# Seven fp64 weight slices get their sign and top exponent bits from ScalarE, and the last expert's 88-row block moves to fourth place

## The chip, the cores and the metric

One core of a Trainium2 chip runs the whole kernel as one program. The metric is the device time of one execution in microseconds (us). A profiled execution has beside it a span, from its first to its last instruction; the profile's times count from the start of the span.

The engines of the core are TensorE (PE, with its weight loads as PEld), VectorE (DVE), ScalarE (ACT), GpSimd (POOL) and SyncE (SP, which here only issues DMAs). Each runs its own instructions in order and waits on semaphores for the others.

## The reference

Three layers follow each other on 2304 tokens of width 512: attention through 32 landmarks with six Newton steps, a dense feed-forward layer with ELU, and a mixture of 8 experts of which each token uses two.

```python
def sm(a, b): ...                      # softmax(scale * a @ b.T)
A = sm(q, k_lm); Bm = sm(q_lm, k_lm); C = sm(q_lm, k)
Z = Bm.transpose(0, 1, 3, 2) / (norm1(Bm) * norminf(Bm) + 1e-06)
for _ in range(6):
    Z = 2 * Z - Z @ Bm @ Z
x = tokens_by_features(A @ Z @ C @ v)            # 2304 x 512
h = x @ w_in                                     # 512 x 2048
x = where(h > 0, h, exp(min(h, 0)) - 1) @ w_out  # 2048 x 512
top2, top2_w = softmax of the two best of x @ w_gate + log1p(exp(x @ w_noise)) * noise
out[mask] += top2_w[mask, k] * (relu(x[mask] @ w1[e]) @ w2[e])   # for e in 8, k in 2
```

w_in and w_out arrive as fp64. The kernel has them as pairs of 32-bit words and makes fp32 numbers of them by bit operations, then splits these into two f16 halves.

## The kernel before

**Order of the work.** Attention of the four batches, the dense layer, the routing and expert 0 are issued from ORDER (L51), a list of tokens written out by hand: each token issues one small step, and each engine executes its instructions in the order in which the tokens issue them. `do` (L1273) reads it. The experts 1 to 7 follow from loops.

**The fp64 slices.** w_in comes in 16 slices of 128x512 numbers (tokens `wi.j` load, `I.j.part` convert), w_out in 16 (`Wl.k` loads, `Wa.k.part` converts, `Wb` splits into f16). `bits32` (L253) gives four parts: part 0 is a ScalarE pass over the low words, which scales them by 2^-29 to integers of three bits (L258, shown as L215, the line of the helper `act`); part 1 is a VectorE pass that shifts the high words left by 3 and masks them into a temporary (L259); part 2 is a second VectorE pass that puts the sign and the top exponent bits from the high word's upper end onto that (L260); part 3 is a GpSimd add of high and low (L261). `wout_a` (L273) and `conv_wi` (L1241) call it. In the profile the tiles are named wi (w_in's slice; wi10 is feature block 1, row block 0) and win (its result), wo and woc (w_out's slice and its temporary), wout (its f16 halves).

**What stands around it.** In the same stretch ScalarE makes the transposed q and k (tile T, from PSUM xp), the landmark means (lm, lT), the exponentials (E, from pc and the maxima mx), and moves between the Newton steps (R). `gmm` (L645, PSUM pg) ends the attention of the first head group; the dense layer's products (L678) follow and keep PE filled from there on.

**The last expert.** Each expert has up to 600 rows, in five blocks: four of 128 and one of 88 (CAP is 600). `e2_mm` (L1154) makes a block's second product in PSUM ey, `e2_rest` (L1192) finishes it. A full block is 24 matmuls of 128x128 weights by 512 columns (L1161). The 88-row block is cut in thirds of 32, 32 and 24 rows, each with a matmul of 384 columns (L1164) and one of 128 (L1167): 144 matmuls and as many weight loads. For expert 7, `last_base` (L1210) first copies the accumulated result to the output (out_dram<-acc, issued by SP) and gathers the rows that expert 7 will change (base<-acc,tk, five DMAs issued by POOL). A `drain` of GpSimd stands ahead of its blocks (L1328). Then the blocks go in the order 4, 0, 1, 2, 3, where 4 is the 88-row block (L1329). Of a full block VectorE makes weight times product plus base (L1199); of the 88-row block ScalarE scales in four passes and VectorE adds the base (L1202). POOL then writes one element as a spacer (L1203) and scatters the rows into the output (L1204). PSUM ey has three buffers.

```python
for j, more in zip((0, 1, 2, 3, 4) if not last else (4, 0, 1, 2, 3), side):
    e2_mm(e, j)
    for g, *a in more:
        g(*a)
    e2_rest(e, j)
```

Of the kernel before, what the change touches and what calls it, by code (L numbers as in the profile page):

```python
# [61 lines left out]
0:asmul.0.G 0:asmax.1 nz.1.0 0:etrans.2 I.6.3 0:uout.2 wi.10 0:etout.0 0:assub.1.V 0:sqout.3 0:asback.0 0:nm.3 0:etout.1
0:uout.3 Wl.7 0:etout.2 I.7.2 0:sqout.4 I.1.2 0:asexp.1 0:nm.4 I.8.0 1:q.1 nz.0.1 0:ashi.0 0:sqout.5 0:cssum I.5.3
Wa.2.1 0:cv cl I.8.1 0:uout.4 Wa.3.2 Wa.2.0 Wa.2.2 wi.14 Wb.1.0.V Wb.1.1.V Wa.2.3 wi.15 I.7.0 0:umm.5 0:assum.1 wi.11
0:cvout I.9.0 1:v 0:uout.5 Wb.5.1.V I.1.3 0:asmul.1.G Wb.0.0.V 0:ybd.V Wa.7.0 1:lmmm.0.0 Wb.2.0.V 0:asback.1 1:xhi.0.0
0:zcv Wa.3.3 I.10.0 I.7.3 0:zout wi.12 1:xlo.0.0 I.8.2 I.15.0 1:lmmm.0.1 0:gmm.0 1:xhi.0.1 0:ashi.1 0:aslo.0.G 1:lmadd.0
F.14 0:ghi.0.0 Wa.7.1 0:aslo.1.G F.8 0:glo.0.0 0:ghi.0.1 0:glo.0.1 Wb.3.0.G I.11.1 L1.0.0 L1.0.1 0:gmm.1 Wa.7.2
1:xlo.0.1 X.0.0 T.0.0.A X.0.1 T.0.1.A I.11.0 1:k.0 Wa.7.3 S.0.0 Wl.8 H.0.0 0:ghi.1.0 L1.0.3 Wb.0.1.V S.0.1 nz.3.1
Wb.2.1.V O.0.0.V H.0.1 nz.0.3 I.10.1 I.9.3 I.11.2 0:ghi.1.1 O.0.1.V 1:xhi.1.0 0:glo.1.0 1:xtr.0.0 L1.0.2 L2.0.0.3 X.0.3
X.0.2 L2.0.0.1 1:xlo.1.0 T.0.2.A T.0.3.A L2.0.0.0 S.0.2 L2.0.0.2 L2.0.1.0 L2.0.1.1 L2.0.1.3 I.11.3 I.8.3 1:lhi.0  # L70
0:glo.1.1 I.13.0 S.0.3 L1.0.4 I.10.2 Wb.7.0.V L1.0.5 Wb.3.1.G 1:llo.0 1:ltr.0 H.0.3 O.0.3.V H.0.2 1:lmsum.1.0.V 1:k.1
L2.0.3.2 X.0.4 O.0.2.G nz.0.2 L2.0.1.2 I.15.1 I.14.1 L2.0.3.0 L2.0.2.1 T.0.4.A Wl.6 Wa.6.1 L2.0.3.1 X.0.5 S.0.4
1:lcp.0.A 1:xtr.1.0 L2.0.3.3 T.0.5.A Wb.7.1.V S.0.5 Wl.9 I.10.3 0:gmm.2 1:lmsum.1.1.V L1.0.6 H.0.4 consts O.0.4.G Wa.6.0
L1.0.7 Wa.6.2 H.0.5 L2.0.2.3 O.0.5.G X.0.6 1:xhi.1.1 0:ghi.2.0 T.0.6.A X.0.7 Wa.8.1 Wa.8.0 Wa.6.3 L2.0.2.0 L2.0.4.2
L2.0.4.1 I.14.0 0:glo.2.0 L2.0.5.0 S.0.6 Wa.8.2 Wb.6.0.V nz.3.0 1:xlo.1.1 L2.0.2.2 I.12.0 L2.0.4.3 1:xtr.1.1 L2.0.4.0
0:ghi.2.1 0:glo.2.1 T.0.7.A Wa.8.3 1:lhi.1 S.0.7 L1.0.8 H.0.7 H.0.6 1:llo.1 Wa.9.1 1:csmm.0 O.0.7.G L2.0.5.2 Wl.10
# [5 lines left out]
1:y0 Wa.12.1 L2.0.9.3 1:sqout.0 I.13.3 Wa.10.1 Wa.10.2 Wa.12.2 T.0.11.A L2.0.9.0 Wa.10.0 T.0.10.A 0:gmm.3 Wa.13.1 S.0.10
0:ghi.3.1 0:ghi.3.0 L2.0.8.1 L2.0.9.2 L2.0.8.3 0:glo.3.0 1:xtr.0.1 Wa.11.0 L2.0.8.2 1:nm.0 0:glo.3.1 Wa.12.3 Wa.10.3
S.0.11 H.0.10 Wl.15 Wa.13.2 1:uout.0 L1.0.13 H.0.11 1:sqout.1 Wb.12.0.G O.0.10.G 1:asmm.1 1:asmax.0 Wb.10.0.V L1.0.12
1:astr.1 O.0.11.G 1:assub.0.V 1:nm.1 1:cssum Wa.11.1 Wb.10.1.V 1:sqout.2 Wa.11.2 1:cv Wl.14 Wa.11.3 Wa.13.3 1:uout.1
1:asmax.1 X.0.12 Wb.12.1.G X.0.13 1:asexp.0 1:nm.2 T.0.12.A L2.0.10.3 Wb.11.0.G 1:sqout.3 fill.0 L2.0.10.2 2:k.0 nz.2.0
1:assub.1.V 1:uout.2 L2.0.10.1 1:asexp.1 L2.0.10.0 T.0.13.A 1:nm.3 1:assum.0 1:sqout.4 S.0.12 Wa.15.1 S.0.13 L1.0.15
1:uout.3 1:asmul.0.G Wb.11.1.G 1:cvout L1.0.14 1:nm.4 H.0.12 1:sqout.5 1:assum.1 2:q.0 L2.0.8.0 L2.0.11.3 Wa.15.2
O.0.12.V Wa.14.1 Wa.15.0 Wb.13.0.V L2.0.12.1 1:uout.4 X.0.14 3:k.0 1:asmul.1.V L2.0.12.3 1:umm.5 Wa.14.2 Wb.13.1.V
H.0.13 Wa.14.0 L2.0.12.0 L2.0.12.2 1:uout.5 Wa.14.3 1:ybd.A 2:q.1 1:asback.1 1:zcv T.0.14.A Wb.14.0.G S.0.14 1:zout  # L90
L2.0.11.1 O.0.13.G L2.0.13.2 Wa.15.3 L2.0.11.0 1:asback.0 L2.0.11.2 H.0.14 1:ashi.0 1:gmm.0 X.0.15 1:aslo.0.V 1:ashi.1
# [1333 lines left out]
```

## Time and profile before

| what | value |
|---|---|
| timed runs | 780.41, 784.45, 786.57 us |
| their median | 784.45 us |
| profiled execution, its own time | 779.94 us |
| its span | 778.3 us |
| what lies around the span | 1.64 us |
| granted TensorE clock over the span | 0.987 of full speed |
| PE busy | 754.0 us, 97% |
| DVE, ACT, POOL busy | 79%, 55%, 36% |

A timeline row gives the start, the duration, the engine and line, the operation with its tiles and shapes, how many instructions run together in the row, and in brackets how long the engine had been idle before and what ended that. "issue" there means that nothing in the profile held the engine back. A windows row gives for a stretch the length, the busy time and number of instructions of each engine, the granted clock, the mean busy share of the 16 DMA engines and their GB/s. A waits row gives the total, the number of times and the longest.

### The profile page before, as it was taken

To read this page: it belongs to the slowest core of one execution; us is meant where nothing else is said; L and a number is where in the kernel's file an instruction comes from. 1 tells how busy PE (TensorE), PEld (TensorE's weight loads), DVE (VectorE), ACT (ScalarE), POOL (GpSimd) and SP (SyncE) were. 2 spreads that over 40 slices of the span, in tenths; PEclk is the share of its full clock that TensorE was granted. 3 is DMA by queue.
4 is the path that set the end of the run, shared out by engine and by line. 5 is a ranking of instruction groups with operands and counts; after the bars stand their busy time and mean duration, and the time that the engine had idled before them with its cause. 6 is when DMAs were issued, how large, how long until landed. Compare 5 with 4: busy or idle time off the path is not lost. (4 is left out here: it accounts for less than half of the span.)

```text
span 778.3 us, 17519 instructions
## 1 busy us (share of the span) xinstructions
PE 754.0 (97%) x6961; PEld 445.0 (57%) x6962; DVE 618.4 (79%) x1352; ACT 427.1 (55%) x820; POOL 281.9 (36%) x302
## 2 busy tenths in 40 slices
...
GB/s 346 265 294 208 173 237 189 185 178 221 110 246 92 190 28 163 124 110 77 100 55 178 117 252 84 230 103 117 226 42 247 96 202 139 71 198 40 145 189 65
DMA packets 136200, 123.19 MB, mean 158 GB/s; under 512 B 102891, under 2 KB 105963, under 8 KB 136016
## 3 DMA queue, kind: packets, MB, share of 16 engines
...
q8 instruction: 56, 0.92, 0.5%
q14 instruction: 32, 0.26, 0.1%
...
## 5 line engine op out<-in xcount | busy, mean ns | idle before, releaser
L718 PE MATMUL y<-wout,g 128*128 128x512 f16 x864 | 205.7, 380 | 0.3 <-DVE g L711 0.2
L1161 PE MATMUL ey<-w,eh 128*128 128x512 f16 x768 | 169.1, 382 | 3.4 <-issue 3.4
L1187 POOL DMA_INDIRECT acc<-eo,tk x35 | 74.2, 2121 | 202.1 <-ACT eo L215 90.5
L718 PEld LDWEIGHTS <-g 128*128 128x128 f16 x864 | 80.7, 98 | 93.8 <-issue 9.0
L1161 PEld LDWEIGHTS <-eh 128*128 128x128 f16 x768 | 75.4, 98 | 94.0 <-issue 6.1
L678 PE MATMUL h<-AT,G 128*128 128x192 f16 (+3 forms) x768 | 108.1, 287 | 1.4 <-DVE e L706 1.2
L711 POOL TENSOR_TENSOR g<-e,g 128x384 f16<-128x384 f32 (+2 forms) x44 | 43.8, 996 | 130.7 <-ACT g L215 116.8
L678 PEld LDWEIGHTS <-G 128*128 128x128 f16 x768 | 63.7, 98 | 43.1 <-issue 5.8
L215 ACT ACTIVATE eh<-c 128x300 f16<-128x300 f32 x112 | 47.7, 453 | 61.1 <-DVE c L1083 60.7
L215 ACT ACTIVATE g<-e 128x384 f16<-128x384 f32 (+2 forms) x96 | 49.4, 519 | 45.9 <-PE y L718 27.1
L215 ACT ACTIVATE e<-h 128x384 f32<-128x384 f32 (+2 forms) x96 | 46.3, 487 | 39.1 <-PE h L678 26.2
L215 ACT ACTIVATE eo<-ey,ws 128x512 f32<-128x512 f32 (+3 forms) x60 | 32.5, 541 | 64.0 <-PE ey L1161 50.9
L706 DVE SCALAR_TENSOR_TENSOR e<-e,h 128x384 f32<-128x384 f32 (+2 forms) x96 | 52.2, 549 | 16.6 <-ACT e L215 14.0
L903 POOL DMA_INDIRECT xs<-rows,pos x36 | 36.9, 1025 | 58.2 <-DVE mcum L887 26.9
L942 DVE SCALAR_TENSOR_TENSOR w<-ew,w 128x1024 f16<-128x1024 f32 x36 | 44.6, 1261 | 14.7 <-ACT w L215 14.7
L1066 PE MATMUL eb<-tx,wpC 128*128 128x300 f16 x336 | 47.4, 291 | 0.0
L1095 DVE SCALAR_TENSOR_TENSOR eh<-c,eh 128x300 f16<-128x300 f32 x112 | 46.2, 466 | 1.0
L711 DVE TENSOR_TENSOR g<-e,g 128x384 f16<-128x384 f32 (+2 forms) x52 | 29.5, 572 | 13.2 <-ACT g L215 13.1
L1066 PEld LDWEIGHTS <-wpD 128*128 128x128 f16 x336 | 32.8, 98 | 10.8 <-issue 0.7
L1066 PEld LDWEIGHTS <-wpB 128*128 128x128 f16 x336 | 32.9, 98 | 10.0
L1066 PEld LDWEIGHTS <-wpC 128*128 128x128 f16 x336 | 32.8, 97 | 10.1
L215 ACT ACTIVATE w<-ew 128x1024 f16<-128x1024 f32 x36 | 37.0, 1050 | 0.2
...
## 6 DMA issues: line engine op xcount, KB each, us to landing
...
wi<-in_moe_w_in_dram SPq DMA_DIRECT2D x16, 512.0 KB, 10.3
...
v<-in_v_dram SPq DMA_DIRECT2D x4, 1152.0 KB, 12.1
out_dram<-acc SPq DMA_DIRECT2D x1, 4608.0 KB, 19.6
...
```

Of the source, the lines that this page charges most:

```text
L215: return A.activation(o, i, f, **kw)
L678: T.matmul(p[:, c0:c0 + n], GT[b, f // 8][:, g, x, fs], AT[b][:, g, y, o:o + n], start=(i == 0), stop=(i == 5))
L706: V.scalar_tensor_tensor(x[1], x[1], x[2], x[0], op0=ALU.mult, op1=ALU.max)
L711: e.tensor_tensor(out=HT[c, f][:, 1], in0=x[1], in1=HT[c, f][:, 0], op=ALU.subtract)
L718: T.matmul(YP[c, t], h[:, x, 128 * t:128 * t + 128], WOUT[f][:, y], start=(f == 0 and i == 0), stop=(f == 15 and i == 2))
L903: n = nc.gpsimd.indirect_dma_start(out=xs[:, :], out_offset=bass.IndirectOffsetOnAxis(ap=R["pos"][:, i // 2, i % 2:i % 2 + 1], axis=0), in ...
L942: V.scalar_tensor_tensor(dst[1][:, ks, :], t, scale, dst[0][:, ks, :], op0=ALU.mult, op1=ALU.subtract)
L1066: T.matmul(p, w_op(e, w, s, k, f), x_op(e, x, t, k), start=(i == 0 and k == 0), stop=(i == 2 and k == 1))
L1095: V.scalar_tensor_tensor(lo, o, 0.0, hi, op0=ALU.max, op1=ALU.subtract)
L1161: T.matmul(p, EH[e, f][:, x, 128 * j:128 * j + 128], W2T[e][y][:, f, :], start=start, stop=stop)
L1187: nc.gpsimd.indirect_dma_start(out=acc[:, :], out_offset=bass.IndirectOffsetOnAxis(ap=TK[e][:live(j), j:j + 1], axis=0), in_=EO[e, j], in_ ...
```

## The change

Two things change. In `bits32`, a slice whose part 0 is called with the argument A gets two more ScalarE passes on the same slice. All three now write 16-bit halves: the low pass writes the lower half of the low word; the two others take the upper half of the high word, cut it with a scale, a bias and rounding to its two top bits, scale them back and write them to the upper half of the low word. The VectorE pass of part 1 then writes its result in place of the high word (for w_out) or into the result (for w_in), with no temporary, and part 2 isn't issued. GpSimd's add is the same. Seven slices are called so: I.2, I.3, I.5 and I.6 of w_in, Wa.0, Wa.1 and Wa.5 of w_out. So ScalarE gets 14 passes more, VectorE 7 fewer; PE, POOL and SP have as many instructions as before. Some tokens of the slices stand elsewhere in ORDER. Besides, the last expert's blocks go in the order 0, 1, 2, 4, 3.

```diff
@@ ORDER, one line of it before and after @@
-0:xtp.1.0.1 0:lmmm.0.1 0:xtp.0.0.2 Wa.4.2 I.0.2 0:xth.0.0.0 I.2.0 0:lmadd.0 I.0.0 0:xth.1.0.2 I.6.1 0:xtp.0.0.1 I.3.1
+0:xtp.1.0.1 0:lmmm.0.1 0:xtp.0.0.2 Wa.4.2 I.0.2 0:xth.0.0.0 I.2.0.A 0:lmadd.0 I.0.0 0:xth.1.0.2 I.6.1 0:xtp.0.0.1 I.3.1
...
@@ bits32 @@
-        return (lambda: act(lo, lo.bitcast(U32), scale=2.0 ** -29),
-                lambda: V.tensor_scalar(tmp, hi, 3, 0x3FFFFFF8, op0=ALU.logical_shift_left, op1=ALU.bitwise_and),
+        x = t.bitcast(U16).rearrange("p (n t) -> p n t", t=4)
+        base = [hi]
+
+        def top():
+
+            act(x[:, :, 1], x[:, :, 3], scale=2.0 ** -14, bias=2.0 ** -15 - 0.5)
+            act(x[:, :, 1], x[:, :, 1], scale=2.0 ** 14)
+
+        def low(e=V):
+            act(lo if e is V else x[:, :, 0], lo.bitcast(U32), scale=2.0 ** -29)
+            if e is A:
+                top()
+                base[0] = hi if dst is None else dst
+
+        return (low,
+                lambda: V.tensor_scalar(base[0] if tmp is None else tmp, hi, 3, 0x3FFFFFF8, op0=ALU.logical_shift_left, op1=ALU.bitwise_and),
                 lambda: V.scalar_tensor_tensor(hi, hi, -0x40000000, tmp, op0=ALU.bitwise_and, op1=ALU.bitwise_or),
-                lambda: G.tensor_tensor(out=hi if dst is None else dst, in0=hi, in1=lo, op=ALU.add)), hi.bitcast(F32)
+                lambda: G.tensor_tensor(out=hi if dst is None else dst, in0=base[0], in1=lo, op=ALU.add)), hi.bitcast(F32)
@@ wout_a; conv_wi gets *e in the same way @@
-    def wout_a(kk, part):
+    def wout_a(kk, part, *e):
         if kk not in WOF:
-            WOF[kk], x = bits32(WO[kk], None, sf.tile([128, 512], I32, tag="cv", bufs=CVB, name=f"woc{kk}"))
+            WOF[kk], x = bits32(WO[kk], None, None if e else sf.tile([128, 512], I32, tag="cv", bufs=CVB, name=f"woc{kk}"))
             WO[kk] = x
-        WOF[kk][part]()
+        WOF[kk][part](*e)
@@ the last expert's blocks @@
-        for j, more in zip((0, 1, 2, 3, 4) if not last else (4, 0, 1, 2, 3), side):
+        for j, more in zip((0, 1, 2, 3, 4) if not last else (0, 1, 2, 4, 3), side):
```

On ScalarE, in the first part, before: the stretch from the second slice of w_in that is converted there (wi10, wi01) past the softmax of the first batch (BB, E) and the transposed queries (T).

```order
L215 ACTIVATE wi10_207<-wi10_207 128x512 [waits DMAHW4_49]
L215 ACTIVATE wi01_135<-wi01_135 128x512 [waits DMAHW7_49]
L215 ACTIVATE T101_261<-xp0111_285 128x384 [waits PE_49]
L215 ACTIVATE BB0_310<-BB0_310 128x64 [waits DVE_49]
L215 ACTIVATE wi10_207<-wi10_207 128x512 [waits DMAHW1_49]
L215 ACTIVATE wout1_346<-wo4_141 128x512 [waits Pool_49]
L215 ACTIVATE E00_358,cs0_357<-pc000_299,mx00_332 128x3x3x32 [waits DVE_49,PE_49]
L215 ACTIVATE E00_358,cs0_357<-pc001_300,mx00_332 128x3x3x32 [waits PE_49]
L215 ACTIVATE T001_366<-xp0010_336 128x384 [waits DMAHW0_49,PE_49]
L215 ACTIVATE wo0_223<-wo0_223 128x512 [waits DMAHW2_49]
L215 ACTIVATE T101_261<-xp0110_328 128x384
L215 ACTIVATE wo5_325<-wo5_325 128x512 [waits DMAHW7_49,Activation_49]
```

The same place now:

```order
L216 ACTIVATE wi10_209<-wi10_209 128x512 [waits DMAHW4_49]
L216 ACTIVATE wi01_135<-wi01_135 128x512 [waits DMAHW7_49]
L216 ACTIVATE wi01_135<-wi01_135 128x512 [waits Activation_49] x2
L216 ACTIVATE T101_260<-xp0111_284 128x384 [waits PE_49]
L216 ACTIVATE BB0_311<-BB0_311 128x64 [waits DVE_49]
L216 ACTIVATE wi10_209<-wi10_209 128x512 [waits DMAHW1_49]
L216 ACTIVATE wi10_209<-wi10_209 128x512 [waits Activation_49] x2
L216 ACTIVATE wout1_349<-wo4_141 128x512 [waits Pool_49]
L216 ACTIVATE E00_361,cs0_360<-pc000_300,mx00_335 128x3x3x32 [waits DVE_49,PE_49]
L216 ACTIVATE E00_361,cs0_360<-pc001_301,mx00_335 128x3x3x32 [waits PE_49]
L216 ACTIVATE T001_369<-xp0010_339 128x384 [waits DMAHW0_49,PE_49]
L216 ACTIVATE wo5_328<-wo5_328 128x512 [waits DMAHW7_49]
```

Two pairs of passes have come in, behind wi01's and the second wi10's, each pass waiting for the one ahead of it; the pass of wo0 has left this place (it now stands earlier, ahead of lm), and two more passes follow wo5's.

On VectorE, at the end of the program, before: the last expert's adds of product and base, by block (eo7_4 is the 88-row block).

```order
L1202 TENSOR_TENSOR eo7_4_10433<-eo7_4_10433,base4_9985 88x512 [waits DMASW7_49,DMASW4_49,Activation_49]
L1199 SCALAR_TENSOR_TENSOR eo7_0_10468<-ey7_0_10443,ws7_9345,base0_9977 128x512 [waits DMASW0_49,DMASW6_49,DVE_49,PE_49]
L1199 SCALAR_TENSOR_TENSOR eo7_1_10499<-ey7_1_10474,ws7_9345,base1_9979 128x512 [waits DMASW5_49,DMASW1_49,PE_49]
L1199 SCALAR_TENSOR_TENSOR eo7_2_10530<-ey7_2_10505,ws7_9345,base2_9981 128x512 [waits DMASW2_49,DVE_49,PE_49]
L1199 SCALAR_TENSOR_TENSOR eo7_3_10561<-ey7_3_10536,ws7_9345,base3_9983 128x512 [waits DMASW6_49,DMASW3_49,PE_49]
```

And now:

```order
L1214 SCALAR_TENSOR_TENSOR eo7_0_10317<-ey7_0_10292,ws7_9349,base0_9981 128x512 [waits DMASW7_49,DMASW0_49,PE_49]
L1214 SCALAR_TENSOR_TENSOR eo7_1_10348<-ey7_1_10323,ws7_9349,base1_9983 128x512 [waits DMASW1_49,DVE_49,PE_49]
L1214 SCALAR_TENSOR_TENSOR eo7_2_10379<-ey7_2_10354,ws7_9349,base2_9985 128x512 [waits DMASW5_49,DMASW2_49,PE_49]
L1217 TENSOR_TENSOR eo7_4_10530<-eo7_4_10530,base4_9989 88x512 [waits DMASW3_49,DMASW4_49,DVE_49,Activation_49]
L1214 SCALAR_TENSOR_TENSOR eo7_3_10565<-ey7_3_10540,ws7_9349,base3_9987 128x512 [waits DMASW6_49,DMASW3_49,PE_49]
```

The 88-row block's add has moved from first to fourth, as have its products on PE, its four passes on ScalarE and its scatter on POOL; which add waits for an earlier scatter (the DMASW semaphores besides its own base) has moved with it.

## Rows read from the trace of the kernel before

**Rows 1.** The page's first part: busy time, share, instructions of each engine.

```profile
PE 754.0 (97%) x6961; PEld 445.0 (57%) x6962; DVE 618.4 (79%) x1352; ACT 427.1 (55%) x820; POOL 281.9 (36%) x302
```

**Rows 2.** Waits of PE: the longest.

```profile
PE ey L1161 <- issue: 3.4, 1, 3.4
```

**Rows 3.** Timeline of the last expert's blocks.

```profile
746.74 0.39 PE L1161 MATMUL ey<-w,eh 128*128 128x512 f16 x1
746.85 1.70 ACT L215 ACTIVATE eo<-ey,ws 88x384 f32<-88x384 f32 x4 [2.43 <-PE ey L1167]
...
750.58 22.36 PE L1161 MATMUL ey<-w,eh 128*128 128x512 f16 x95 [3.44 <-issue]
...
754.22 18.23 PEld L1161 LDWEIGHTS <-eh 128*128 128x128 f16 x85 [0.16 <-issue]
754.30 0.69 DVE L1202 TENSOR_TENSOR eo<-eo,base 88x512 f32<-88x512 f32 x1 [9.37 <-issue]
...
758.47 0.09 POOL L1203 MEMSET spacer<- 1x1 f32 x1 [18.63 <-issue]
...
762.79 0.75 DVE L1199 SCALAR_TENSOR_TENSOR eo<-ey,ws,base 128x512 f32<-128x512 f32 x1 [4.60 <-DMA out_dram<-eo,tk]
...
772.98 0.75 DVE L1199 SCALAR_TENSOR_TENSOR eo<-ey,ws,base 128x512 f32<-128x512 f32 x1 [4.43 <-PE ey L1161]
774.01 0.98 POOL L1204 DMA_INDIRECT out_dram<-eo,tk  x1 [4.15 <-DVE eo L1199]
```

**Rows 4.** Windows: the 88-row block, the pause behind it, and what follows.

```profile
742.60:746.74 4.14, 4.14 (x145) 4.03 (x145) 2.19 (x6) 0.83 (x2) 0.00 (x0) 1.00 1.17 364
746.74:750.50 3.76, 0.39 (x3) 0.10 (x1) 0.00 (x0) 1.66 (x4) 0.00 (x0) 1.00 0.67 211
750.50:754.30 3.80, 3.72 (x10) 1.41 (x11) 0.00 (x0) 0.00 (x0) 0.00 (x0) 0.55 0.34 123
```

**Rows 5.** The page's DMA queues: packets, MB, share; one of the instruction queues.

```profile
q8 instruction: 56, 0.92, 0.5%
```

**Rows 6.** DMA queues and transfers from 726 to 747.5 us, all kinds.

```profile
q1 hardware_dynamic: 95, 4.67, 62.8%
q0 software_dynamic: 199, 0.39, 11.9%
q14 instruction: 3, 0.02, 0.4%
issues: line engine op xcount, KB each, median us to landing
out_dram<-acc SPq DMA_DIRECT2D x1, 4608.0 KB, 19.6
base<-acc,tk POOLq DMA_INDIRECT x5, 17.9
```

**Rows 7.** The same view from 747.5 to 749 us.

```profile
q8 instruction: 1, 0.02, 3.7%
```

**Rows 8.** Groups of ScalarE, 0 to 50 us, shapes apart: busy, mean ns.

```profile
L215 ACT ACTIVATE wi<-wi 128x512 int32<-128x512 uint32 x10 | 6.7, 692 | 5.1 <-DMA wi<-in_moe_w_in_dram 5.1
...
L215 ACT ACTIVATE ET<-pe 96x512 f32<-96x512 f32 x3 | 1.7, 591 | 0.0
```

**Rows 9.** The same for VectorE.

```profile
L260 DVE SCALAR_TENSOR_TENSOR wi<-wi,win 128x512 int32<-128x512 int32 x9 | 6.5, 725 | 0.0
```

**Rows 10.** Timeline of the first part: where ScalarE waits, and the first gmm.

```profile
13.50 0.68 ACT L215 ACTIVATE wo<-wo 128x512 int32<-128x512 uint32 x1 [1.66 <-DMA wo<-in_moe_w_out_dram]
...
21.32 0.42 ACT L215 ACTIVATE lm<-k 128x256 f32<-128x256 f32 x1 [3.42 <-DVE k L345]
...
25.36 0.26 ACT L215 ACTIVATE BB<-BB 128x64 f32<-128x64 f32 x1 [0.54 <-DVE BB L452]
...
27.73 0.65 ACT L215 ACTIVATE E<-pc,mx 128x288 f32<-128x288 f32 x1 [0.97 <-DVE mx L518]
...
34.48 0.22 ACT L215 ACTIVATE R<-nb 128x64 f32<-128x64 f32 x1 [1.16 <-DVE R L571]
...
44.32 0.69 ACT L215 ACTIVATE wi<-wi 128x512 int32<-128x512 uint32 x1 [1.06 <-DMA wi<-in_moe_w_in_dram]
...
54.14 1.09 PE L645 MATMUL pg<-win,Z 64*32 64x512 f32 x16
```

More of the change, by code (lines that the diff above doesn't have):

```diff
@@ L62 @@
[L62 to L76, printed above, removed]
@@ L82 @@
[L82 to L91, printed above, removed]
@@ new lines @@
+wi.14 Wb.1.0.V Wb.1.1.V Wa.2.3 wi.15 I.7.0 0:umm.5 0:assum.1 wi.11 0:cvout I.9.0 1:v 0:uout.5 Wb.5.1.V I.1.3 0:asmul.1.G
+Wb.0.0.V 0:ybd.V Wa.7.0 1:lmmm.0.0 Wb.2.0.V 0:asback.1 1:xhi.0.0 0:zcv Wa.3.3 I.10.0 I.7.3 0:zout wi.12 1:xlo.0.0 I.8.2
+I.15.0 1:lmmm.0.1 0:gmm.0 1:xhi.0.1 0:ashi.1 0:aslo.0.G 1:lmadd.0 F.14 0:ghi.0.0 Wa.7.1 0:aslo.1.G F.8 0:glo.0.0
+0:ghi.0.1 0:glo.0.1 Wb.3.0.G I.11.1 L1.0.0 L1.0.1 0:gmm.1 Wa.7.2 1:xlo.0.1 X.0.0 T.0.0.A X.0.1 T.0.1.A I.11.0 1:k.0
+Wa.7.3 S.0.0 Wl.8 H.0.0 0:ghi.1.0 L1.0.3 Wb.0.1.V S.0.1 nz.3.1 Wb.2.1.V O.0.0.V H.0.1 nz.0.3 I.10.1 I.9.3 I.11.2
@@ new lines @@
+0:ghi.1.1 O.0.1.V 1:xhi.1.0 0:glo.1.0 1:xtr.0.0 L1.0.2 L2.0.0.3 X.0.3 X.0.2 L2.0.0.1 1:xlo.1.0 T.0.2.A T.0.3.A L2.0.0.0
+S.0.2 L2.0.0.2 L2.0.1.0 L2.0.1.1 L2.0.1.3 I.11.3 I.8.3 1:lhi.0 0:glo.1.1 I.13.0 S.0.3 L1.0.4 I.10.2 Wb.7.0.V L1.0.5
+Wb.3.1.G 1:llo.0 1:ltr.0 H.0.3 O.0.3.V H.0.2 1:lmsum.1.0.V 1:k.1 L2.0.3.2 X.0.4 O.0.2.G nz.0.2 L2.0.1.2 I.15.1 I.14.1
+L2.0.3.0 L2.0.2.1 T.0.4.A Wl.6 Wa.6.1 L2.0.3.1 X.0.5 S.0.4 1:lcp.0.A 1:xtr.1.0 L2.0.3.3 T.0.5.A Wb.7.1.V S.0.5 Wl.9
+I.10.3 0:gmm.2 1:lmsum.1.1.V L1.0.6 H.0.4 consts O.0.4.G Wa.6.0 L1.0.7 Wa.6.2 H.0.5 L2.0.2.3 O.0.5.G X.0.6 1:xhi.1.1
@@ new lines @@
+T.0.9.A L2.0.7.1 1:bnorm L1.0.10 Wl.12 Wb.9.1.V 1:csexp.1 L2.0.6.2 S.0.9 I.14.3 1:nmm H.0.8 I.12.3 1:etrans.0 1:nval
+L2.0.6.1 Wa.12.0 1:etrans.1 L1.0.11 Wl.13 H.0.9 1:etout.1 1:etout.0 O.0.9.V Wb.8.1.V Wa.13.0 I.13.2 X.0.11 L2.0.9.1
+I.15.3 1:etrans.2 O.0.8.G 1:sqmm.0 1:etout.2 X.0.10 1:y0 Wa.12.1 L2.0.9.3 1:sqout.0 I.13.3 Wa.10.1 Wa.10.2 Wa.12.2
+T.0.11.A L2.0.9.0 Wa.10.0 T.0.10.A 0:gmm.3 Wa.13.1 S.0.10 0:ghi.3.1 0:ghi.3.0 L2.0.8.1 L2.0.9.2 L2.0.8.3 0:glo.3.0
+1:xtr.0.1 Wa.11.0 L2.0.8.2 1:nm.0 0:glo.3.1 Wa.12.3 Wa.10.3 S.0.11 H.0.10 Wl.15 Wa.13.2 1:uout.0 L1.0.13 H.0.11
@@ new lines @@
+X.1.1 T.1.1.V 2:xhi.0.1 S.1.1 1:glo.1.0 H.1.1 L2.0.15.1 O.1.1.G L2.0.15.0 1:glo.1.1 L2.0.15.2 YA.0.0 L1.1.2 YA.0.2
+L2.0.15.3 S.1.0 1:gmm.2 X.1.2 YV.0.2 T.1.2.A S.1.2 H.1.0 L1.1.4 O.1.0.V 1:ghi.2.0 2:k.1 YV.0.0 2:lmsum.1.1.G H.1.2 X.1.4
+O.1.2.V T.1.4.A L1.1.5 L2.1.0.0 1:ghi.2.1 S.1.4 L2.1.0.1 H.1.4 1:glo.2.0 L1.1.3 X.1.3 fill.2 2:xtr.1.0 YA.0.1 YA.0.3
+2:lhi.0 L2.1.2.1 1:glo.2.1 O.1.4.V 1:gmm.3 T.1.3.V L2.1.2.0 S.1.3 YV.0.3 H.1.3 X.1.5 L1.1.6 YV.0.1 2:llo.0 L2.1.4.1
+T.1.5.A 2:lmsum.1.0.G S.1.5 L2.1.4.0 O.1.3.G nz.0.0 X.1.6 RT.0.0 L2.1.1.1 T.1.6.V L1.1.8 1:ghi.3.1 H.1.5 1:ghi.3.0
@@ new lines @@
+L2.2.8.1 L2.2.10.1 L1.2.13 X.2.11 2:uout.3 2:sqout.4 L2.2.9.2 3:llo.0 T.2.11.A S.2.11 2:nm.4 H.2.12 2:asback.0 2:uout.4
+2:sqout.5 facc.2 L2.2.9.0 2:umm.5 L2.2.10.0 L1.2.14 H.2.11 2:uout.5 O.2.12.G 2:ashi.0 2:ybd.V 2:zcv O.2.11.V L2.2.11.2
+PD.0.7 X.2.13 2:zout L2.2.12.0 2:gmm.0 X.2.14 3:xtr.1.0 2:ghi.0.1 L2.2.11.0 2:assum.1 T.2.14.A 2:asmul.1.V 3:ltr.0
+T.2.13.V 3:lmsum.1.1.G RS.1.0 S.2.13 L2.2.10.2 L2.2.11.1 2:asback.1 2:aslo.0.V 2:ghi.0.0 H.2.13 L2.2.12.2 2:ashi.1 3:v
+3:lcp.0.A S.2.14 2:glo.0.0 L1.2.15 PD.1.6 H.2.14 2:aslo.1.G 2:glo.0.1 O.2.14.V 3:csmm.0 O.2.13.G L2.2.12.1 X.2.15
@@ new lines @@
+3:etout.0 L1.3.5 L2.3.1.2 3:etout.1 X.3.4 T.3.4.V L2.3.2.2 L2.3.1.1 2:gmm.2 S.3.4 L1.3.6 RG.2 H.3.4 O.3.3.G RS.1.2
+2:ghi.2.1 2:glo.2.1 O.3.4.V 3:llo.1 L2.3.2.1 RA.2 L2.3.3.2 X.3.6 L2.3.3.1 T.3.6.V X.3.5 3:ltr.1 2:ghi.2.0 L2.3.4.0
+3:xtr.0.1 T.3.5.V P.0.0.0 L2.3.2.0 S.3.6 3:cv RB.2 3:lcp.1.A 3:bmm L1.3.7 3:xlo.0.0 RC.2 S.3.5 H.3.5 3:cvout P.0.7.0
+2:glo.2.0 3:bmax O.3.5.V 3:bex X.3.7 T.3.7.A 2:gmm.3 L2.3.5.2 RD.2 3:bnorm L2.3.3.0 L2.3.4.1 S.3.7 3:nmm L1.3.9
+3:xtr.0.0 2:ghi.3.1 RE.2 PD.1.2 H.3.7 L2.3.4.2 O.3.7.V L2.3.7.2 2:ghi.3.0 2:glo.3.0 3:nval RK.2 RF.2 H.3.6 2:glo.3.1
@@ new lines @@
+3:sqout.5 3:uout.4 L2.3.8.0 3:umm.5 H.3.12 S.3.11 H.3.11 L1.3.14 3:assub.0.V O.3.11.G L1.3.13 3:uout.5 3:ybd.A L2.3.9.0
+3:asexp.0 3:asmul.1.G 3:zcv O.3.12.G L2.3.9.2 L2.3.11.1 X.3.13 3:assum.0 3:asback.1 3:zout T.3.13.A 3:gmm.0 3:ashi.1
+S.3.13 L2.3.11.2 H.3.13 X.3.14 O.3.13.V 3:ghi.0.0 L2.3.12.1 T.3.14.V 3:asmul.0.G 3:asback.0 L2.3.11.0 L2.3.12.2
+3:ghi.0.1 RS.2.3 3:ashi.0 3:aslo.1.V 3:aslo.0.V L2.3.12.0 L1.3.15 X.3.15 S.3.14 3:glo.0.0 H.3.14 L2.3.13.2 O.3.14.G
+T.3.15.A 3:glo.0.1 3:gmm.1 RS.2.2 L2.3.14.0 S.3.15 L1.4.1 3:ghi.1.0 L2.3.14.1 3:ghi.1.1 L1.4.0 H.3.15 X.4.0 T.4.0.V
```

189 lines of the change are left out of this document (90 added, 99 removed).

## The prediction, on record before the run

> **What bounds the kernel now.** I read the page's first part first: PE is busy for 754.0 of the span's 778.3 us [rows 1], so only what makes PE wait, or runs behind its last product, can move the end. The waits of PE come next. The longest of the whole program is 3.4 us put down to "issue", on L1161, the last expert's second products [rows 2]; that is one of the two places that the change touches. The timeline shows it: the 88-row block's products end, one product of block 0 runs at 746.74, and the next 95 start at 750.58 after 3.44 us of idle [rows 3]. ScalarE's four passes on the 88-row block are done by 748.55, and nothing in the kernel makes block 0's second product wait for them.
>
> What PE lacks there I take to be its own code. Queue q8 moved 0.92 MB in 56 packets [rows 5], 16.4 KB each; PE's 6961 + 6962 instructions [rows 1] over 56 are 249 per packet, so I read q8 as PE's code. From 726 to 747.5 us the list of queues has no q8 at all, while the copy out_dram<-acc of 4608 KB took 19.6 us to land [rows 6] and the DMA engines stood at a share of 1.17 [rows 4]. One q8 packet came between 747.5 and 749 [rows 7], and PE ran again at 750.58. The 88-row block is hungry: it and the first product used 145 matmuls and 145 loads, 290 instructions, in 4.14 us [rows 4], where a full block has 48 in some 5 us. [...]
>
> **The tail, step by step.** At full clock 85 products took 18.23 us, 0.2145 each; 95 would take 20.38, and took 22.36 [rows 3]. So the pause costs 3.44 and the slow clock behind it 1.98, together 5.42 us. In the new order blocks 0, 1 and 2 come first: 144 instructions in 72 x 0.2145 = 15.44 us, so until 742.60 + 15.44 = 758.04. The code on hand reached 290 instructions past 742.60; 146 of these are left for the 88-row block, used up at about 758.04 + 146/290 x 4.14 = 760.1. The packet that came late for 746.74 lies well ahead of that, with the copy over at about 752. I therefore take pause and slow clock as gone: PE ends at 742.60 + 4.14 + 96 x 0.2145 = 767.3, some 0.2 more for the joints, against 772.94. That is **-5.4 us**.
>
> What could be late next: block 0's add needs its gathered base; the 88-row block's add in the old order started at 754.30, behind the last of the gathers [rows 3, 6], so none comes later than that. Block 4 is the fourth to use one of three PSUM buffers, and block 0's is free by 754.30 + 0.75 = 755.1, ahead of 758.04. POOL's first spacer comes at 758.47 in either order (the drain ahead of it), and the add that waits for the first scatter's landing then comes at 762.79 [rows 3]; in the new order that is block 2's, 4.6 us ahead of PE's end. The 88-row block ends on PE at 762.4; 1.70 us of ScalarE and 0.69 of VectorE [rows 3] bring it to about 765, its scatter to 766.2, and block 3's scatter, the last, is due at 768.5. So the last block still sets the end and is a full one as before: 0.75 us of add, 0.98 of scatter, and what follows [rows 3], unchanged.
>
> **The front, step by step.** Seven VectorE passes go, 725 ns each in w_in's group [rows 9]: 7 x 0.725 = 5.1 us of VectorE, which nothing on PE waited for, so I count them at nothing; were they on the path, that would be the gain. The cost is ScalarE's: 14 passes more. Their form, 16-bit elements 8 bytes apart, is in no row. The nearest is the low pass itself, 4-byte elements 8 bytes apart, 692 ns [rows 8]; as each pass waits for the one ahead of it, I put them 0.71 apart. Below, I take 591 ns, the shortest row of 512 elements [rows 8]; above, twice the 692, 1.38, should half words written into a word cost a pass of their own. I take 0.71, near the nearest row.
>
> Slice I.2's two passes lie ahead of the wait at 13.50 (1.66 us idle), and Wa.0's three in the 3.42 us of idle ahead of lm at 21.32 [rows 10]: nothing, though the latter only if its slice has landed by about 19 us; at twice the price they would end a good 1 us late. The other five slices bring ten passes between 23.2 and 34.5 us, where ScalarE is nearly full: 10 x 0.71 = 7.1, less 0.7 for Wa.0's first pass, which has left this stretch. Of these 6.4 us the waits there swallow 0.54 (BB), 0.97 (E) and 1.16 (R, a Newton step) [rows 10], together 2.67. What is left, 3.7, moves the Newton steps, whose products PE can't start earlier, and is cut once more by the 1.06 us that ScalarE waits for a slice's DMA at 44.32 [rows 10]: 2.7. Two VectorE instructions now queue behind ScalarE's longer series (Wa.5's shift, the f16 split of w_out); behind them stand the next Newton operations, for a few tenths. I take **+3.0 us** at gmm (54.14 [rows 10]); from there PE is filled, and the delay is carried to the end. At 0.591 the same sum gives 5.9 - 0.7 - 2.67 - 1.06 = +1.5, at 1.38 it gives 13.8 - 4.4 = +9.4.
>
> [...]
>
> **The sum.** -5.4 + 3.0 = -2.4 us: the profiled execution would go from 779.94 to 777.5. That execution is the lowest of four; the three timed ones are 780.41, 784.45 and 786.57, so a median of a few runs lies higher. I put -2.4 on the median of all four, (780.41 + 784.45) / 2 = 782.4: **780.0 us**.
>
> **Rivals.**
>
> *A: the pause stays.* If it is not the code's lateness but something that comes with the switch from 288 narrow products to full ones, or if half of the 88-row block, now in fourth place, finds its code missing in turn, the 5.4 us are not gained, only moved. For it: the pause stands right at that switch, and the trace has no line that names its cause. Against it: the seven earlier experts have the same block and no such wait among PE's, and q8's one packet fits. Then only the front counts: 782.4 + 3.0 = 785.4.
>
> [...]
>
> *B: the half-word passes are dear.* Writing 16 bits into 32-bit words costs ScalarE twice: +9.4 at the front, - 5.4 at the tail, so slower, 782.4 + 4.0 = 786.4. For it: no row shows such a pass, and a series in which each waits for the last. Against it: the strided pass of 4 bytes costs no more than other passes. It decides from 10p - 4.4 = 5.4, so from 0.98 us per pass.
>
> *C: the front costs nothing.* PE's waits in the first 55 us have other causes too, DMAs among them, and VectorE, freed of 5.1 us, reaches its own steps earlier. For it: ScalarE's waits for DMAs at 13.50 and 44.32 [rows 10]. Against it: ten passes between 23 and 34.5 us, where ScalarE waits for 2.67 us in all. Then -5.4 alone: 777.0.
>
> **How the numbers follow.** Forecast 0.55, A 0.17, B 0.10, C 0.18. The range: C's 777.0 less the spread of runs at the lower end, B's 786.4 with it at the upper, so 772 to 788. A measurement of this kernel can tell about 1%, 7.8 us, from no change; most of the forecast, all of A and most of B lie within. Faster by more than 1% needs C, or the forecast with the spread on its side: 0.17. Slower by more needs B with the spread: 0.06. Same: 0.77.
>
> **What would show it.** Right: in the changed profile PE has no "issue" wait on L1176 (the new number of L1161's line), the granted clock of the tail is 1.00, and PE's last product ends some 5.3 us before the span does, as now; ten passes of about 0.7 us more between 23 and 38 us on ScalarE; gmm at about 57.1 instead of 54.14. Wrong: a pause within or behind the 88-row block (A); half-word passes at 1 us or more and gmm beyond 60 (B); gmm at 54 to 55 (C); or POOL's or VectorE's last wait ending on a scatter instead of PE.

## The result, and the profile after

The changed kernel took 793.97 us (median of four, 792.93 to 794.48), the kernel before beside it 782.61 us: a ratio of 1.0145, 95% interval 1.0108 to 1.0183. So it is slower by some 11 us, where the prediction said 2.4 us faster on a median of 782.4, with 788 as the upper end. In the profiles the span went from 778.3 to 792.5 us.

The waits of PE in the changed kernel (total, times, longest), for the one row of [rows 2]:

```profile
PE xp L412 <- ACT T L216: 5.6, 2, 3.4
PE pa L438 <- ACT T L216: 4.0, 1, 4.0
...
PE pe L550 <- ACT E L216: 2.3, 1, 2.3
...
PE l1b L377 <- ACT lm L216: 1.4, 1, 1.4
...
PE ey L1182 <- issue: 0.7, 2, 0.4
```

The 3.4 us of "issue" on the last expert are gone. In their place stand waits on ScalarE, 13.3 us together in the first four rows, all in the first 55 us; before, only the wait for E was among them, with 0.9 us. What ScalarE did there shows in its groups from 0 to 56 us, shapes apart (busy, mean ns, idle before), which answer to [rows 8]:

```profile
L216 ACT ACTIVATE wi<-wi 128x512 uint16<-128x512 uint16 x8 | 10.8, 1346 | 0.3
L216 ACT ACTIVATE wo<-wo 128x512 uint16<-128x512 uint16 x6 | 8.1, 1344 | 0.2
...
L216 ACT ACTIVATE wi<-wi 128x512 uint16<-128x512 uint32 x4 | 5.4, 1350 | 2.9 <-DMA wi<-in_moe_w_in_dram 2.9
L216 ACT ACTIVATE wo<-wo 128x512 uint16<-128x512 uint32 x3 | 4.1, 1356 | 1.1 <-DMA wo<-in_moe_w_out_dram 1.1
...
L216 ACT ACTIVATE wi<-wi 128x512 int32<-128x512 uint32 x3 | 2.1, 704 | 0.0
```

The 14 added passes took 1.35 us each, not 0.71. And the low pass of the seven slices, which the change did not add but made to write 16 bits, went from 0.69 to 1.35 as well; the slices that still write 32 bits are at 0.70. So 21 passes are dear, not 14.

The timeline of the same stretch shows a slice holding ScalarE for 4.1 us, and the Newton step R behind it starting with no idle time of ScalarE ahead of it, where [rows 10] has 1.16 us; then the first product of gmm, which stood at 54.14:

```profile
40.19 4.09 ACT L216 ACTIVATE wo<-wo 128x512 uint16<-128x512 uint32 x3
...
44.99 4.10 ACT L216 ACTIVATE wi<-wi 128x512 uint16<-128x512 uint32 x3
48.84 0.30 ACT L216 ACTIVATE R<-nb 128x64 f32<-128x64 f32 x1
...
67.15 1.09 PE L660 MATMUL pg<-win,Z 64*32 64x512 f32 x16
```

So gmm is 13.0 us late. At the other end, the timeline of the last expert, for [rows 3]:

```profile
760.59 15.70 PE L1176 MATMUL ey<-w,eh 128*128 128x512 f16 x72
...
778.25 0.11 PEld L1182 LDWEIGHTS <-eh 128*32 128x32 f16 x2 [0.29 <-issue]
...
778.98 0.23 PE L1182 MATMUL ey<-w,eh 128*32 128x128 f16 x1 [0.35 <-issue]
...
779.71 0.23 PE L1182 MATMUL ey<-w,eh 128*32 128x128 f16 x1 [0.35 <-issue]
...
781.83 5.35 PE L1176 MATMUL ey<-w,eh 128*128 128x512 f16 x24
```

The windows of blocks 0 to 2, of the 88-row block and of block 3 (columns as in [rows 4]):

```profile
760.40:776.20 15.80, 15.80 (x75) 7.09 (x73) 4.30 (x10) 0.99 (x3) 0.09 (x1) 1.00 0.53 173
776.20:781.80 5.60, 4.83 (x145) 4.04 (x144) 0.71 (x1) 0.00 (x0) 2.17 (x4) 1.00 0.25 97
781.80:787.20 5.40, 5.38 (x26) 2.27 (x24) 0.73 (x2) 1.66 (x4) 2.13 (x4) 1.00 0.26 82
```

The clock stays at 1.00, and from the first product to the end of the last the expert takes 787.18 - 760.59 = 26.6 us, against 772.94 - 742.60 = 30.3 before. But the 88-row block takes 5.6 us instead of 4.14: PE halts three times in its middle, and no wait on another engine stands ahead of a halt. The two ends make 13.0 - 3.7 = +9.3 of the span's 14.2 us; the remaining 4.9 lie between gmm and the last expert (688.5 us before, 693.4 after). The runs below show that the passes do not make these.

### The profile page after: what moved, and what is told of

Same layout as the page of the kernel before. It is cut to its first block, busy times and chain, and to the rows that moved or that the text cites. A ratio compares the mean times of both kernels' runs of the same rounds, so it can differ in the third digit from the quotient of the medians.

```text
span 792.5 us, 17527 instructions
## 1 busy us (share of the span) xinstructions
PE 758.0 (96%) x6961; PEld 446.5 (56%) x6962; DVE 615.0 (78%) x1345; ACT 449.4 (57%) x834; POOL 282.4 (36%) x302
## 5 line engine op out<-in xcount | busy, mean ns | idle before, releaser
L1176 PE MATMUL ey<-w,eh 128*128 128x512 f16 x768 | 167.4, 379 | 0.0
L216 ACT ACTIVATE e<-h 128x384 f32<-128x384 f32 (+2 forms) x96 | 46.5, 487 | 40.3 <-PE h L693 26.6
```

The lines of the kernel that those rows point to most:

```text
L216: return A.activation(o, i, f, **kw)
L1176: T.matmul(p, EH[e, f][:, x, 128 * j:128 * j + 128], W2T[e][y][:, f, :], start=start, stop=stop)
```

## The experiments

Theory T: the ScalarE passes cost the front some 13 us because of their price, and the block order gains by itself.

**e1_order_alone.** The block order without the passes:

```diff
-        for j, more in zip((0, 1, 2, 3, 4) if not last else (4, 0, 1, 2, 3), side):
+        for j, more in zip((0, 1, 2, 3, 4) if not last else (0, 1, 2, 4, 3), side):
```

> Only the last expert's block order of the change (0, 1, 2, 4, 3), no ScalarE pass added. Theory T: the block order gains by itself, because PE no longer stands for 3.4 us behind the 88-row block and no half-clock stretch follows; in the changed kernel the last expert's products took 26.6 us instead of 30.3, so about 4 us faster than before, 778 to 779 where before has 782.6, the profile's span near 774; a remainder of the pause (0.5 to 2 us) inside the 88-row block. Rival U: the gain in the changed kernel came from the late start of its last expert (other transfers beside it), the block order alone gains nothing: within 1 us of before.

774.22 us beside 777.56 (another chip, on which the kernel before takes 5 us less): ratio 0.9957, interval 0.9931 to 0.9982. The order gains 0.43%, 3.3 us, alone; U falls. In its profile the windows of blocks 0 to 2, the 88-row block and block 3 show no halt at all, 25.1 us together:

```profile
740.40:756.10 15.70, 15.70 (x74) 6.98 (x72) 3.87 (x8) 0.83 (x2) 0.00 (x0) 1.00 0.57 186
756.10:760.20 4.10, 4.10 (x145) 4.03 (x144) 0.00 (x0) 0.00 (x0) 1.64 (x4) 1.00 0.06 19
760.20:765.70 5.50, 5.42 (x29) 2.27 (x24) 1.48 (x3) 1.66 (x4) 3.04 (x6) 1.00 0.39 143
```

A packet on q8 starts at 745.74 here, 5.3 us after the expert's first product and so hardly sooner than before (748.24 against 742.61, 5.6 us). PE doesn't stand for it: until then it has met only full blocks, 48 instructions in 5.2 us each, where the 88-row block has 288 in 4.1.

**e2_passes_alone.** The changed kernel with the blocks in the old order (4, 0, 1, 2, 3).

> Only the ScalarE passes of the change, the last expert's blocks in the old order (4, 0, 1, 2, 3). Theory T: the passes alone cost 13 us up to the first gmm, some 2 us where ScalarE stands before a transposed landmark copy near 190 us, and some 2 us at narrow products near 280 us; with the old block order the pause of 3.4 us is back: about 798 us where before has 782.6, span near 796. Rival U: without the new block order the late products give back what the middle lost: 792 to 794, no slower than the changed kernel.

791.66 beside 777.56 us, ratio 1.0178 (1.0128 to 1.0227), so by the ratio 13.8 us slower. gmm starts at 66.89, the pause is back:

```profile
66.89 1.09 PE L660 MATMUL pg<-win,Z 64*32 64x512 f32 x16
...
762.71 22.15 PE L1176 MATMUL ey<-w,eh 128*128 128x512 f16 x95 [2.70 <-issue]
```

The two parts multiply to 1.0178 x 0.9957 = 1.0134, the whole has 1.0145: the times agree with two separate effects of opposite sign. They don't tell this kernel from the changed one, whose interval overlaps (1.0108 to 1.0183), so against U speaks the profile, with its pause, and not the time. What T got wrong is the middle: from gmm to the last expert it is 688.6 us here, as in before, although all the passes are there. So the changed kernel's 4.9 us in the middle are not the passes'.

**e3_low_word.** The low pass of the seven slices writes the whole word again:

```diff
-            act(lo if e is V else x[:, :, 0], lo.bitcast(U32), scale=2.0 ** -29)
+            act(lo, lo.bitcast(U32), scale=2.0 ** -29)
```

> The changed kernel, but the low pass of the seven slices writes the whole low word again (32 bits), and only the two passes behind it write 16 bits; the result is the same. Theory T: the width of the output sets the price, 1.35 us for 16 bits and 0.69 for 32: seven passes go from 1.35 to 0.69, some 3 us less at the first gmm (near 64 instead of 67.15), 3 to 4 us faster than the changed kernel, about 790. Rival V: the seven slices' passes are dear because each waits for the one ahead: the low pass stays at 1.35 or the others stay and nothing moves: 793 to 794.

784.26 beside 777.56 us, ratio 1.0090 (1.0062 to 1.0118). gmm comes at 63.43, 3.5 us sooner than in e2. ScalarE's groups:

```profile
L216 ACT ACTIVATE wi<-wi 128x512 uint16<-128x512 uint16 x8 | 10.8, 1346 | 0.3
...
L216 ACT ACTIVATE wi<-wi 128x512 int32<-128x512 uint32 x9 | 6.1, 695 | 3.0 <-DMA wi<-in_moe_w_in_dram 3.0
```

The low pass fell to 0.695 with the series and its waits unchanged: at this spacing of 8 bytes the price follows the width of the output. V falls. Against the changed kernel's ratio the time gained 0.55%, 4.3 us, where 3 to 4 were expected; the intervals don't tell these apart.

**e4_probe.** The kernel before with ScalarE passes on a scratch tile behind its end, nine forms twice.

```diff
+                act(pw[:, :, 0], pw[:, :, 1])
+                act(ph[:, :, 0], ph[:, :, 3])
+                act(pw[:, :, 0], ph[:, :, 3])
+                act(ph[:, :, 0], pw[:, :, 1])
+                act(dh, ph[:, :, 3])
...
```

Here pw is the tile as 32-bit words 8 bytes apart, ph as 16-bit halves 8 bytes apart, dh dense 16-bit.

> The kernel before with 18 ScalarE passes of 128x512 on a scratch tile behind its end, nine forms twice; only their durations count, its time is longer by them. Theory T (a 16-bit output in the middle of words costs twice): the forms with 16-bit output 8 bytes apart 1.35 us, those with 32-bit output 0.69 whatever their input. Rival V: a 16-bit input costs twice, so 16-bit to 32-bit is 1.35 and 32-bit to 16-bit 0.69. Rival W: any 16-bit integer output costs twice, dense ones too.

ScalarE's groups (busy, mean ns), the first five passes in order and the seventh, 16-bit halves 4 bytes apart, each from a window that holds it alone:

```profile
L216 ACT ACTIVATE probe<-probe 128x512 int32<-128x512 int32 x1 | 0.7, 659 | 22.8 <-DVE probe L1337 22.8
...
L216 ACT ACTIVATE probe<-probe 128x512 uint16<-128x512 uint16 x1 | 1.3, 1335 | 0.0
...
L216 ACT ACTIVATE probe<-probe 128x512 int32<-128x512 uint16 x1 | 0.7, 652 | 0.0
...
L216 ACT ACTIVATE probe<-probe 128x512 uint16<-128x512 int32 x1 | 1.3, 1337 | 0.0
...
L216 ACT ACTIVATE probe<-probe 128x512 uint16<-128x512 uint16 x1 | 0.7, 687 | 0.0
...
L216 ACT ACTIVATE probe<-probe 128x512 uint16<-128x512 uint16 x1 | 0.8, 821 | 0.0
```

Input does not matter: 16-bit halves 8 bytes apart are read at 652 ns into 32-bit words and at 687 into dense halves. A 16-bit output 8 bytes apart costs 1334 to 1337, whatever is read. A dense 16-bit output costs 629 to 687, so V and W both fall. T holds for 8 bytes; 16-bit output 4 bytes apart took only 821 and 819 ns, so it is width and spacing together that cost. Why they do, no run shows.

This kernel has the old block order, and in it the pause behind the 88-row block was only 1.47 us, with its 95 products at full clock (1.00). The second row below is the window behind the pause; the third is the same window of e2, where the pause was 2.70 us and the granted clock 0.59:

```profile
746.99 20.68 PE L1162 MATMUL ey<-w,eh 128*128 128x512 f16 x95 [1.47 <-issue]
...
746.90:750.90 4.00, 3.91 (x19) 1.80 (x20) 0.00 (x0) 0.03 (x1) 0.00 (x0) 1.00 0.65 229
...
762.60:766.40 3.80, 3.69 (x11) 1.41 (x12) 0.00 (x0) 0.00 (x0) 0.00 (x0) 0.59 0.51 161
```

So the pause is not of one size, and its size goes with the q8 packet. In before, e2 and e4 the packet started 5.6, 4.8 and 3.5 us after the expert's first product (at 748.24, 760.26 and 744.53), and the pause took 3.44, 2.70 and 1.47 us. From the packet's start to the products behind the pause it is 2.3 to 2.5 us in all three. The packet in the DMA views of e2 from 760 to 761 and of e4 from 744 to 745:

```profile
q8 instruction: 1, 0.02, 5.5%
...
q8 instruction: 1, 0.02, 5.5%
```

**e5_no_copy.** Old block order, without the copy.

```diff
-        nc.sync.dma_start(out, acc[:NT])
```

> The kernel before, old block order, without the copy out_dram<-acc: rows of the output that expert 7 doesn't write are left unwritten. Theory T (PE's code comes late because the 4608 KB copy fills the DMA engines): the q8 packet that came 5.6 us after the 88-row block's start comes within 2 us of it, no pause behind the block, the last expert's products take 25 to 26 us (30.3 in the profile of before, 29.4 with the passes alone), and the time falls by 2 to 6 us. Rival A (the pause belongs to the switch from narrow products to full ones): products still take 28 to 30.5 us with a pause behind the 88-row block.

779.22 beside 783.27 us, ratio 0.9951 (0.9928 to 0.9975). There is no pause behind the block: its 96 products run through, and the q8 packet starts at 747.79, ahead of the expert's first product at 748.16. The timeline, the DMA view from 747 to 749, and the windows:

```profile
752.29 20.89 PE L1161 MATMUL ey<-w,eh 128*128 128x512 f16 x96
```

```profile
q0 software_dynamic: 23, 0.05, 6.7%
q8 instruction: 1, 0.02, 3.6%
```

```profile
748.10:752.40 4.30, 4.30 (x146) 4.14 (x146) 2.35 (x6) 0.83 (x3) 0.09 (x1) 1.00 0.00 0
752.40:773.30 20.90, 20.79 (x96) 9.18 (x95) 3.01 (x5) 1.66 (x4) 4.30 (x8) 1.00 0.14 48
```

The switch from 288 narrow instructions to full products is still there and costs nothing: rival A, as a matter of the switch, falls.

**e6_shifted_code.** Old block order, copy in place, 64 one-column products in the first part: 128 more PE instructions ahead of all that follows. If q8's packets are PE's code, as I read them, each then starts at another place in the program, and by T of e5 the pause goes if one starts early enough.

```diff
+        if n == 16 and not SHIFT:
+            SHIFT.append(1)
+            for _ in range(64):
+                T.matmul(WARM[0][:32, :1], hot[:, :32], hot[:, :1], start=True, stop=True)
```

> [...] Rival A: the pause of 3 us stays behind the 88-row block, products 28 to 30.5 us.

778.08 beside 783.27 us, ratio 0.9939 (0.9917 to 0.9961), though the kernel does more. gmm is not late (53.42), and the 88-row block runs at a DMA share of 1.08, nearly as loaded as in before (1.17), without a pause behind it. The windows, and the q8 packet in the DMA view from 740.5 to 741.5:

```profile
745.50:749.90 4.40, 4.40 (x146) 4.14 (x146) 2.56 (x7) 0.93 (x3) 0.00 (x0) 1.00 1.08 365
749.90:770.70 20.80, 20.68 (x96) 9.17 (x94) 2.92 (x5) 1.56 (x4) 4.39 (x9) 1.00 0.29 102
...
q8 instruction: 1, 0.02, 8.1%
```

The same block, the same copy and the same switch are there; what moved is the packet's start, at 740.92, 4.6 us ahead of the expert's first product instead of 5.6 behind it. The three profiles with a pause come from other chips or jobs than e5 and e6, so a pause that this chip never has isn't excluded by the profiles alone. But both kernels gain 4 to 5 us on the kernel before beside them, and in the three profiles that have it the pause grows with the packet's lateness, microsecond for microsecond. So in the old block order the pause is a matter of when the q8 packet starts. That it carries PE's instructions is my reading; the trace calls its queue only "instruction". Not all of e6's gain need come from it: from gmm to the last expert it has 692.1 us where e5 has 694.4.

**e7_after_again.** The changed kernel beside before on one chip.

> The changed kernel again, beside the kernel before on the same chip. Its profile had 693.4 us between the first gmm and the last expert's products, where all others had 688.3 to 688.7; the rest came from ScalarE standing 3.8 us at a landmark copy and PE halting at narrow products. Theory T: these two belong to that one execution; now 688.3 to 689 us, span 787 to 789, ratio to before 1.012 to 1.016. Rival X: they come with the 14 passes and the shifted instructions: again 692 to 694.

795.16 beside 783.27 us, ratio 1.0158 (1.0129 to 1.0188). The middle is long again, 694.5 us, against what T expected. But so it is in e5 (694.4) and in e10 below (695.3), which have none of the passes. In these profiles ScalarE stands before the same landmark copy; here e10, where the product pl was done at 172.24:

```profile
171.85 0.39 PE L367 MATMUL pl<-ident,lm 128*128 128x128 f16 x4
...
175.61 0.60 ACT L215 ACTIVATE lT<-pl 128x512 f16<-128x512 f16 x1 [3.08 <-PE y L718]
...
176.26 0.56 PE L431 MATMUL pa<-T,lT 64*32 64x288 f16 x24 [1.75 <-ACT lT L215]
```

So neither T's words ("belong to that one execution") nor X hold. All four profiles of e1 to e4, on one chip, have 688.3 to 688.7 us, with and without the passes; all seven of e5 to e11, on two others, have 691.4 to 696.3. The long middle is a matter of the chip or of the run, and what makes it is open. In e6 and e11 ScalarE hardly stands there (0.29 and 0.48 us), and their middles are still 692.1 and 691.4, so that wait is not all of it.

**e8_two_slices.** The new block order, and only I.2 and Wa.0 converted in 16-bit passes.

> Block order 0, 1, 2, 4, 3 and only two of the seven slices (I.2 and Wa.0, which lie ahead of ScalarE's long waits) converted by ScalarE in 16-bit passes; the other five as before. Theory T: 13 us of the changed kernel come from the five slices between 23 and 50 us, the two cost 1 to 2 us (Wa.0's passes end after lm's operand is there): gmm at 54 to 56, time 1 to 3 us faster than before. Rival Y: the delay is made by any of the slices (the DMA that comes later into a slot, the first transposes): 4 us or more at gmm, slower than before.

783.42 beside 783.27 us, ratio 1.0014 (0.9993 to 1.0034): beside the order alone (0.9957, e1 and e10, on other chips) the two slices eat its whole gain. gmm is at 55.01, within what T said and 1.2 us behind e5, which ran on the same chip. G behind it (the tile between gmm and the dense layer's products) is late too, so that these products start 2.9 us later than in e5, at 58.97 instead of 56.03:

```profile
58.97 3.06 PE L693 MATMUL h<-AT,G 128*128 128x512 f16 x12 [1.58 <-ACT G L216]
```

The 88-row block has its halts again (26.7 us for the expert). T expected faster; it was no change. The prediction's "nothing" for these two slices does not hold at this price.

**e9_price_as_assumed.** The changed kernel with the two added passes, and the low pass as in e3, writing 32-bit words.

```diff
-            act(x[:, :, 1], x[:, :, 3], scale=2.0 ** -14, bias=2.0 ** -15 - 0.5)
-            act(x[:, :, 1], x[:, :, 1], scale=2.0 ** 14)
+            act(lo, x[:, :, 3], scale=2.0 ** -14, bias=2.0 ** -15 - 0.5)
+            act(lo, lo, scale=2.0 ** -14)
```

> The changed kernel with all three passes of the seven slices writing whole 32-bit low words; sign and top bits of these slices are left out of the weights. So the passes have the same number, order and waits as in the change, at the price that the prediction assumed, 0.65 to 0.70 us. Theory T (only the price was wrong): gmm comes about 3 us later than without the passes, 56 to 58 us, the tail is as in the changed kernel, and the time is within 0.4% of before, -0.3% by the prediction's own sum. Rival Z (the sum itself missed waits, whatever the price): gmm at 60 us or later and 0.5% or more slower.

782.92 beside 782.65 us, ratio 0.9997 (0.9976 to 1.0019). The passes took 669 to 687 ns, and gmm starts at 56.30, where the prediction had 57.1:

```profile
L216 ACT ACTIVATE wi<-wi 128x512 int32<-128x512 int32 x4 | 2.7, 678 | 0.1
L216 ACT ACTIVATE wi<-wi 128x512 int32<-128x512 uint16 x4 | 2.7, 669 | 0.1
```

With the price that the prediction assumed, the passes delay gmm as it said, and the time is that of the kernel before, within T's 0.4%. Z falls. But the -0.3% of the prediction's own sum (780.0 on 782.4, a ratio of 0.9969) lies outside the interval, whose lower end is 0.9976. Beside e10, the order alone on the same chip (780.48 us), the passes at this price cost 2.4 us, where the prediction had 3.0; what is missing is gain of the order, 2.2 us here and not 5.4.

**e10_order_again** and **e11_order_and_shift**, in the same job: the block order alone, and with e6's 64 products.

> The new block order alone, again, to stand beside the next two kernels on one chip. Theory T: 0.4 to 0.6% faster than before; the last expert's products 25 to 26.7 us. Whether PE halts a little inside the 88-row block (26.7 in the changed kernel, 25.1 in the first run of this one) belongs to the chip or execution and not to the passes: if it is the chip, this run has whatever the other two have.

> The new block order and the 64 one-column products that shift the bounds of PE's code packets by 128 instructions. Theory T: the two cures remove the same pause, so together they give no more than one of them: 0.4 to 0.7% faster than before, products 25 to 26.7 us. Rival: two separate gains, which add up to 1.0% or more.

e10: 780.48 beside 782.65 us, ratio 0.9957 (0.9933 to 0.9981), as in e1. This time the 88-row block halts (5.55 us instead of 4.10; 26.6 us for the expert, 25.1 in e1), with no pass in the kernel: the halts in the changed kernel are not the passes' either. e11: 780.05 us, ratio 0.9952 (0.9923 to 0.9980); 27.0 us for the expert, where T had at most 26.7. Both cures together give what one gives. The block order alone, without the ScalarE passes, is a version that beats both kernels, in two jobs by 0.43%; e6's ratio of 0.9939 is not told apart from it. The window of e10's 88-row block:

```profile
762.60:768.15 5.55, 4.77 (x145) 3.99 (x144) 0.39 (x1) 0.00 (x0) 2.26 (x5) 1.00 0.26 97
```

## Why the prediction was wrong

**The price of a pass: the step that failed.** The prediction put the 16-bit passes at 0.71 us, "near the nearest row", which was the low pass with its 4-byte elements 8 bytes apart. It chose that row by the spacing, and at this spacing it is the width of what is written that decides: 1335 ns against 652 for the same input (e4). The dense and the 32-bit passes of e4 took 629 to 687, so its lower end of 591 and its 0.71 lie close to those forms and not to this one. Rival B had it at 1.38, at a chance of 0.10.

**A pass not counted.** The prediction priced the added passes alone and took the low pass as it was, although the diff makes it write 16 bits. Five such passes lie in the full stretch: 5 x 0.66 = 3.3 us. e3 measures 3.5 at gmm. This is why even B's +9.4 fell short. By the prediction's own sum with both put right, 10 x 1.35 + 3.3 - 0.7 - 2.67 - 1.06 = 12.4 us; measured 13.0 between the first two profiles, 14.7 between e1 and e2 on one chip. With these 12.4 for the 3.0 the forecast would have been 782.4 + 12.4 - 5.4 = 789.4 us, and with the 3.3 us that the order gave in e1 for the 5.4, 791.5; measured 793.97. That leaves some 2 us, for which the two slices below are the nearest term.

**The rest of the front's sum: borne out.** Ten passes, the waits that swallow 2.67 and 1.06, gmm 3 us late at 0.71: e9 shows 56.30, against 51.7 to 54.1 in seven profiles without the passes (54.14 before; 52.20, 52.29, 53.81, 53.42, 51.65 and 52.37 in e1, e4, e5, e6, e10 and e11), so 2.2 to 4.7 late, and the time 2.4 us more than e10's. No run tests the single waits that it subtracts.

**VectorE's seven passes at nothing: not contradicted.** In e9 they are gone, and the order and the delay of the front leave no gain to explain; no run took them away alone.

**Two slices at nothing: wrong at the true price.** e8: they cost about what the order gains. The prediction had said that at twice the price Wa.0's passes would end a good 1 us late; gmm is 1.2 us behind e5 in e8. This 1 us is missing from its sum at 1.38.

**The tail: the lateness borne out, the term too large.** The pause goes with the start of a q8 packet: in the old order it stands where the packet starts 3.5 to 5.6 us after the expert's first product (before, e2, e4), and is absent where it starts 0.4 us ahead of it without the copy (e5) or 4.6 us ahead with it (e6). That this packet is PE's code is still a reading, from the prediction's 249 instructions per packet, and how the copy delays it no run shows. But -5.4 us was the pause and the slow clock of one profile: 3.44 us with a granted clock of 0.55 behind it there (1.00 again from 754.30 to 773.00), 2.70 with 0.59 in e2, 1.47 with 1.00 in e4, all in the old order. And the 88-row block in its new place halts for some 1.5 us in the changed kernel and in e7 to e11, not in e1 and e3. What makes these halts is open: a q8 packet starts inside that block in e1 and e3 too, at 758.34 and 769.69, and PE doesn't halt there. Timed, the order gives 3.3 and 2.2 us by the medians, 0.43% by both ratios.

**What bounds, and the rivals.** PE's waits did decide, and the last full block still ended the kernel. A fell as a matter of the switch. Its second half, that the 88-row block finds its own code missing in its new place, is not shown: 1.5 us of halts stand there in six profiles and none in two. C fell. B's mechanism held, and both its signs came, passes of more than 1 us (1.35, beyond its point of 0.98) and gmm beyond 60 (67.15); its 786.4 was too low, for it lacked the low passes and the two slices, and took the tail at 5.4.
